# An attention and snake kernel on one core: reciprocals of the first chunk on VectorE, one load on another queue, two reordered stages

## The chip, the core and the metric

The kernel runs on one core of a Trainium2 chip. The metric is the device time in microseconds of one execution. A core has five engines that run their own instruction queues in order and wait for each other by semaphores: TensorE (PE; its weight loads are shown apart as PEld), VectorE (DVE), ScalarE (ACT), GpSimd (POOL) and SyncE (SP). SyncE, ScalarE and GpSimd also start DMA transfers. PSUM, where TensorE writes, is used here as four pairs of banks, called slots 0 to 3.

## What is computed

The reference, cut to what matters. The types are float32.

```python
# q, k, v: (8, 12, 448, 64)
def rmsnorm(x, g):
    return x / np.sqrt(np.mean(x * x, axis=-1, keepdims=True) + 1e-06) * g
q_n, k_n = rmsnorm(q, g_q), rmsnorm(k, g_k)
scores = np.matmul(q_n, k_n.transpose(0, 1, 3, 2)) / np.sqrt(64)
attn = np.exp(scores - np.max(scores, axis=-1, keepdims=True))
attn = attn / (np.sum(attn, axis=-1, keepdims=True) + 1e-09)
x = np.matmul(attn, v).transpose(0, 2, 1, 3).reshape(8 * 448, 12 * 64)
# w_in: (768, 2048), w_out: (2048, 768), alpha: (2048,)
h = x @ w_in
g = h + np.sin(alpha * h) ** 2 / (alpha + 1e-09)
out = g @ w_out
```

## The kernel before

The eight batches run one after the other. The 12 heads of a batch make three chunks of four heads; chunk numbers in the code count through all batches (0, 1, 2 are batch 0's, 3, 4, 5 batch 1's). For a chunk, q and k are loaded (`load_qk`), squared, summed (`reduce`), turned into an inverse root by Ln and Exp on ScalarE (`rsqrt`), scaled (`scale`), and transposed on TensorE (`pe_transpose`, chunks 0 to 2) or by DMA (`transpose`). A batch has 21 score tiles, seven for each chunk: TensorE multiplies (L357), ScalarE takes the exponential (L360), and the result goes to `expT`. Sums over the keys are matmuls with ones into `av` (L416, or L404 for the first chunk of later batches); values are matmuls with `vb`. The reciprocal of the sums, `rec`, is made on ScalarE as Exp of minus Ln (L431 and L432, L423 to L425 in later batches). VectorE multiplies values by `rec` into `xT` (L440).

`first_product` multiplies `xT` by `w_in` into `hps` (L468, 96 matmuls): 24 matmuls for the first four of 16 tiles, in the order of `xT`'s six parts 0, 1, 2, 4, 3, 5, and then six for each tile. ScalarE takes the sine (L446) and half of the squares (L451), GpSimd the other squares (L449), and VectorE writes `g_sb` (L454). `second_product` multiplies `g_sb` by `w_out` into `ops`. For all batches but the last its steps (L548, eight quarter-size matmuls each) are spread as fillers through the next batch's attention; for the last batch it runs by itself at the end (L526, 128 matmuls of 384 columns), with copies to `osb` on VectorE (L532) and, for the last half unit, ScalarE (L534), and stores (L516).

The order of the work is written out by hand in strings. `STAGE_0` is batch 0's, `STAGE_1` batch 1's, `STAGE_N` that of all later ones. Each has three parts: the tokens of the attention, the order in which PSUM slots are taken, and the tasks that stand beside the first product (-1 is ahead of its fifth part, i behind its i-th pair of tiles). Tokens, with a chunk's number within the batch (3, 4 and 5 are the next batch's) and often w (0 for q, 1 for k) and a head pair: `q` square, `u` sum of squares, `g` multiply q by the norm weights, `r` inverse root, `k` scale, `p` transposes on TensorE, `t` by DMA, `l` load q and k, `D` a small copy on GpSimd that waits for a chunk's load, `S` one score tile (`S4` with four warm-up matmuls ahead, L352), `o`, `v`, `x`, `y`, `z` a number of key tiles of the ones of the first chunk, its values, the ones, low and high values of the other two chunks, `G` and `L` the spread of the norm weights and of alpha over the partitions, `V`, `W`, `O` loads of v, `w_in` and `w_out` on GpSimd's queue, `F` (also written as a number) and `f` a filler of the current or of the next half tile of the second product.

A batch-0 `rec` of the first chunk is made when the last `o` is through; for chunks 0 to 3 the inverse root lies in a PSUM slot until the scaling is done.

Of the kernel before, what the change touches and what calls it, by code (L numbers as in the profile page):

```python
# [17 lines left out]
try:  # L18
# [12 lines left out]

STAGE_0 = (
    (
        "q000 u000 q010 G q011 q001 u010 g00 u011 r01 g01 D1 u001 k01 r00 k00 q11 u11 O00 q10 V00 p012 "
        "W01 q20 p00 g1 u10 r1 q21 u20 V01 g2 S4 V02 S k11 l3 k10 S1 S1 S4 W00 W02 S u21 r2 p1 S2 S q31 "
        "S3 k21 q30 k20 D2 S S3 o3 l4 g3 S W10 W12 o1 o3 p2 u30 l5 S3 u31 S1 S W11 S4 v7 S S S q40 S S x5 "
        "y3 q41 u41 x1 g4 z4 u40 x1 L r4 y4 O01 q50 z3 r3 O10 "
    ),
    "012311203203310210213023012310321032021321302",
    {-1: 'u50 O11 k30', 0: 'D4 k401', 1: 'k411', 2: 'q51', 3: 'k31 k400 u51', 5: 'k410', 7: 'g5 V12', 8: 't3 V10 V11 t4 l6 l7'},  # L40
)
STAGE_1 = (
    (
        "4 r2 f f k20 1 f f 2 k21 S 1 q31 1 t2 S 1 S 2 S q30 2 S 2 S S 3 f S 3 S 1 f S 1 S 1 u31 2 l5 g3 "
        "S u30 o1 o6 1 r3 V10 2 S f q41 1 f 2 S 2 S 2 q40 S u41 1 v1 v1 S v3 V12 S k31 q50 v2 u40 S 2 S "
        "V11 g5 S z4 x7 y7 r4 z3 g4 k30 "
    ),
    "1320201203203013133213130101301231203123",
    {-1: 'u50 t3', 0: 'k41', 2: 'k40', 5: 'q51', 6: 'l6 t4', 8: 'u51 l7'},
)  # L50
STAGE_N = (
    (
# [16 lines left out]
def kernel(  # L69
# [23 lines left out]
    nc = tc.nc  # L93
    B, H, S, D = q.shape
    D_MODEL = H * D
    D_FF = moe_w_in.shape[1]
    P = 128
    KT = D_MODEL // P
    MT = D_FF // P
# [7 lines left out]
    HALF = D_MODEL // 2  # L107
# [85 lines left out]
            queue.dma_start(out=g_rows[:, i], in_=src.rearrange("(a d) -> a d", a=1))  # L193

    load_qk(0, nc.scalar)
    load_qk(1, nc.scalar)
    load_qk(2)
    nc.gpsimd.dma_start(out=small, in_=moe_alpha.rearrange("(mt p) -> mt p", p=P))
    nc.scalar.preload_act_table_set(EXP_LN)
# [15 lines left out]
    w_out_sb = wpool.tile([P, MT, D_MODEL], BF16)  # L215
    g_sb = gpool.tile([P, MT, 2 * S], BF16)
# [168 lines left out]
    def attend(b, what, tiles=range(NJ)):  # L385
# [3 lines left out]
        kind, both = what.split()  # L389
        both = both == "1"  # L390
        if tiles[0] == 0:
            avs[what] = bank_pair("av")
        av = avs[what]
        pre = presums.get(b) if what == "ones 0" else None
        last = 1 if pre else NJ - 1
        halved = what == "ones 0" and b > 0
# [22 lines left out]
        if kind == "ones":  # L419
            rec = recs[both] = pre.t if pre else rpool.tile([P, 2, S], F32, tag="rec", name="rec")  # L420
            if halved:
                cols = [slice(0, S // 2), slice(S // 2, S)]
                nc.scalar.activation(rec[:, :, cols[0]], av[:, :, cols[0]], ACT.Ln)  # L423
                nc.scalar.activation(rec[:, :, cols[1]], rec[:, :, cols[0]], ACT.Exp, scale=-1.0)
                nc.scalar.activation(rec[:, :, cols[0]], rec[:, :, cols[0]], ACT.Exp, scale=-1.0)  # L425
                for pp in range(2):
                    for qh in range(2):
                        src, dst = (slice((2 * pp + x) * 32, (2 * pp + x) * 32 + 32) for x in (qh, 1 - qh))
                        nc.vector.reduce_sum(rec[dst, :, cols[qh]], rec[src, :, cols[qh]].unsqueeze(3), axis=AX.X)  # L429
            for k in () if halved else ((0, 1), (1, 2)) if both and b == 0 else ((0, 2),):  # L430
                nc.scalar.activation(rec[:, slice(*k)], av[:, slice(*k), :S], ACT.Ln)  # L431
                nc.scalar.activation(rec[:, slice(*k)], rec[:, slice(*k)], ACT.Exp, scale=-1.0)  # L432
            give_back(avs.pop(what))
        else:
            if b not in xT:
                xT[b] = xpool.tile([P, KT, S], BF16, tag="xT", name="xT")
            first = 0 if not both else 2 if kind == "low" else 3
            for k in (slice(0, 1), slice(1, 2)) if both and b == 0 else (slice(0, 2),):
                kts = slice(first + k.start * (1 + both), first + (k.stop - 1) * (1 + both) + 1, 1 + both)
                nc.vector.tensor_mul(xT[b][:, kts, :], av[:, k, :S], recs[both][:, k])  # L440
            give_back(avs.pop(what))
# [56 lines left out]
    def second_product(b):  # L498
# [19 lines left out]
        for unit in units:  # L518
            st = {}

            def whole_array(m, unit=unit, st=st):
                if m == 0:
                    st["ps"] = bank_pair("ops")
                for k, (i, half) in enumerate(unit):
                    c0 = odd * (S + REST) + i * P if i < NT else NT * P
                    nc.tensor.matmul(st["ps"][:, k, :HALF], g_sb[:, m, c0:c0 + P],  # L526
                                     w_out_sb[:, m, half * HALF:(half + 1) * HALF], start=(m == 0), stop=(m == MT - 1))
                if m == MT - 1:
                    n, i = len(unit), unit[0][0]
                    osb = opool.tile([P, 2, HALF], F32, tag="osb", name="osb")  # L530
                    cut = HALF // 2 if unit is units[-1] else HALF
                    nc.vector.tensor_copy(osb[:, :n, :cut], st["ps"][:, :n, :cut])  # L532
                    if cut < HALF:
                        nc.scalar.copy(osb[:, :n, cut:], st["ps"][:, :n, cut:HALF])  # L534
                    give_back(st["ps"])
                    store(osb[:, :n], i, slice(unit[0][1] * HALF, (unit[-1][1] + 1) * HALF))

# [143 lines left out]
```

## Time and profile before

| what | us |
|---|---|
| median of 8 runs | 409.04 (408.04 to 409.95) |
| the profiled execution | 409.95 |
| its span | 408.2 |
| TensorE busy | 391.5 (96%) |
| ScalarE busy | 315.5 (77%) |
| GpSimd busy | 283.6 (69%) |
| VectorE busy | 240.2 (59%) |

The granted TensorE clock is full in all 40 slices of the span. The chain of work that ended last consists of TensorE for 86% of the span; of its lines, L468 has 34% and L548 29%. The other engines appear in the chain mainly in the first 45 us: loads of q and k, GpSimd's squares, VectorE's scalings.

How to read it: times in the timeline are from the span's start. A line gives start, length, engine, source line, the instruction and its tiles, and in brackets how long the engine stood idle before it and what ended that. A line can merge several instructions (x6); its length is then that of the whole run of them. DMA lines give size and the time from issue to landing.

### The profile page before, as it was taken

What the parts mean: (1) busy time and instruction counts of PE and PEld (TensorE: products, weight loads), DVE (VectorE), ACT (ScalarE), POOL (GpSimd) and SP (SyncE); (2) the same over time, 40 slices, a digit from 0 to 9 for tenths busy, and PEclk for the clock granted to TensorE, in tenths of its full rate; (3) what the DMA queues carried; (4) which work ended last, traced back from release to release, by engine and by line L of the source; (5) the groups of instructions that cost most, each with busy time, mean ns of one, the idle gap of its engine ahead of it and who ended that gap; (6) DMA issues with size and microseconds to landing.
All of it is one profiled execution on the core that took longest, in us unless ns stands there. A gap on an engine that the chain in (4) does not pass through costs nothing.

```text
span 408.2 us, 15186 instructions
## 1 busy us (share of the span) xinstructions
PE 391.5 (96%) x6742; PEld 237.6 (58%) x6742; DVE 240.2 (59%) x363; ACT 315.5 (77%) x475; POOL 283.6 (69%) x268
## 2 busy tenths in 40 slices
PE   0998999999999999999999999999999999999995
PEld 0345467655676556755676556755667556765563
DVE  3956675746784476738584575836685484544411
ACT  4797889878997788958898678958898678977500
POOL 4989879897869789588877779597895774004300
PEclk9999999999999999999999999999999999999999
DMA  7999999766186935699076933979046901520022
GB/s 263 194 252 248 211 203 254 198 124 221 31 149 180 161 101 88 181 171 177 3 134 168 200 114 70 178 169 203 3 95 176 166 2 34 95 61 1 2 77 77
DMA packets 67686, 55.44 MB, mean 136 GB/s; under 512 B 41493, under 2 KB 63013, under 8 KB 67621
## 3 DMA queue, kind: packets, MB, share of 16 engines
q1 hardware_dynamic: 56226, 40.97, 43.2%
q0 software_dynamic: 10432, 11.81, 19.1%
q10 hardware_dynamic: 962, 1.70, 1.1%
q8 instruction: 52, 0.85, 0.9%
q14 instruction: 14, 0.11, 0.1%
HBM read 45.62 MB, written 11.01 MB: 139 GB/s over the span
## 4 chain that ended last, share of the span: by engine, by line
PE 86%; POOL 3%; DVE 3%; DMA 3%; issue 2%; ACT 1%; ACTq 0%; SPq 0%; POOLq 0%
PE hps L468 34%; PE ops L548 29%; PE av L416 9%; PE sc L357 7%; PE ops L526 5%; DMA qk<-in_q_dram 2%; POOL sq L281 2%; PE av L404 1%; DMA qk<-in_k_dram 1%; DVE qkn L309 1%; ACT expT L360 1%; DVE rec L429 1%; DVE ms L290 1%; POOL qk L286 1%; POOL w_out_sb L248 1%
## 5 line engine op out<-in xcount | busy, mean ns | idle before, releaser
L360 ACT ACTIVATE expT<-sc 128x896 bf16<-128x896 f32 x168 | 143.6, 917 | 7.1 <-PE sc L357 6.4
L548 PE MATMUL ops<-w_out_sb,g_sb 64*64 64x384 bf16 x3072 | 148.1, 323 | 0.0
L468 PE MATMUL hps<-xT,w_in 128*128 128x448 bf16 x768 | 146.8, 353 | 0.9 <-DVE alpha_sb L232 0.5
L468 PEld LDWEIGHTS <-w_in 128*128 128x128 bf16 x768 | 74.5, 98 | 72.7 <-issue 4.1
L454 DVE SCALAR_TENSOR_TENSOR g_sb<-s,inv_alpha_sb,hps 128x448 bf16<-128x448 f32 x128 | 81.0, 676 | 59.2 <-POOL s L449 58.7
L548 PEld LDWEIGHTS <-g_sb 64*64 64x64 bf16 x3072 | 92.2, 107 | 36.8 <-issue 3.8
L449 POOL TENSOR_TENSOR s<-s 128x448 f32<-128x448 f32 x64 | 59.7, 933 | 64.8 <-ACT s L446 43.0
L446 ACT ACTIVATE s<-hps,alpha_sb 128x448 f32<-128x448 f32 x128 | 74.0, 627 | 37.8 <-PE hps L468 37.4
L309 POOL TENSOR_TENSOR qkn<-qk,inv 128x448 bf16<-128x448 f32 x80 | 73.0, 940 | 24.5 <-issue 17.1
L281 POOL TENSOR_TENSOR sq<-qk 128x896 f32<-128x896 f32 x44 | 73.4, 1680 | 6.0 <-DVE ms L290 2.9
L357 PE MATMUL sc<-qkT 64*64 64x448 bf16 x672 | 60.2, 355 | 0.7 <-ACT expT L360 0.3
L286 POOL TENSOR_TENSOR qk<-qk,gg 128x896 f32<-128x896 f32 (+1 forms) x25 | 50.5, 2021 | 3.1 <-ACT g_sb L278 2.5
L554 DVE COPY osb<-ops 128x384 f32<-128x384 f32 x48 | 26.7, 556 | 38.6 <-PE ops L548 34.2
L290 DVE TENSOR_REDUCE ms<-sq 128x14 f32<-128x896 f32 x44 | 46.4, 1077 | 5.0 <-POOL sq L281 5.0
L440 DVE TENSOR_TENSOR xT<-av,rec 128x896 bf16<-128x896 f32 (+1 forms) x26 | 25.5, 1013 | 25.8 <-ACT rec L432 21.1
L451 ACT ACTIVATE s<-s 128x448 f32<-128x448 f32 x64 | 36.9, 577 | 3.0 <-DVE g_sb L454 0.7
L416 PE MATMUL av<-expT,vb 64*32 64x448 bf16 (+1 forms) x1120 | 38.1, 350 | 0.0
L357 PEld LDWEIGHTS <-qkT 64*64 64x64 bf16 x672 | 21.8, 107 | 13.6 <-issue 6.1
L555 DVE TENSOR_TENSOR osb<-osb,ops 128x384 f32<-128x384 f32 x48 | 26.6, 554 | 1.7
L416 PEld LDWEIGHTS <-vb 64*32 64x32 bf16 (+1 forms) x1120 | 20.1, 95 | 11.4 <-issue 2.2
L429 DVE TENSOR_REDUCE rec<-rec 32x448 f32<-32x448 f32 x28 | 17.1, 610 | 9.7 <-ACT rec L425 9.4
L526 PE MATMUL ops<-w_out_sb,g_sb 128*128 128x384 bf16 x128 | 21.0, 326 | 0.0
(52 smaller groups left out, 184.8 us busy)
## 6 DMA issues: line engine op xcount, KB each, us to landing
qk<-in_q_dram SPq DMA_DIRECT2D x23, 448.0 KB, 5.2
qk<-in_k_dram SPq DMA_DIRECT2D x22, 448.0 KB, 5.5
out_dram<-osb SPq DMA_DIRECT2D x45, 192.0 KB, 2.9
w_out_sb<-in_moe_w_out_dram POOLq DMA_DIRECT2D x4, 768.0 KB, 12.4
w_in<-in_moe_w_in_dram POOLq DMA_DIRECT2D x6, 512.0 KB, 12.2
vb<-in_v_dram POOLq DMA_DIRECT2D x16, 168.0 KB, 7.4
vb<-in_v_dram POOLq DMA_DIRECT2D x8, 224.0 KB, 4.9
out_dram<-osb SPq DMA_DIRECT2D x14, 96.0 KB, 4.0
```

What stands on the lines that cost most here:

```text
L281: nc.gpsimd.tensor_mul(st.sq[w], qk[ci][:, w], qk[ci][:, w])
L286: nc.gpsimd.tensor_mul(x, x, gg.to_broadcast([P, len(heads) * NJ, D]))
L290: nc.vector.reduce_sum(st.ms[:, w, rows], st.sq[w][:, rows], axis=AX.X)
L309: eng.tensor_mul(n[:, :, hi, :], x[:, hi], inv[:, hi].unsqueeze(2).to_broadcast([P, NJ, D]))
L357: nc.tensor.matmul(sc[o:o + 64, hi, :S], qkt[r, 1, j * REST:(j + 1) * REST], qkt[r, 0, :], start=True, stop=True)
L360: nc.scalar.activation(expT[c, j], sc[:, :, :S], ACT.Exp, scale=SCALE)
L416: nc.tensor.matmul(av[o, k, :S], w, x[r, hi, :], start=(j == 0), stop=(j == last))
L446: nc.scalar.activation(s1, hps, ACT.Sin, scale=alpha_sb[:, m, :])
L449: nc.gpsimd.tensor_mul(s2, s1, s1)
L454: nc.vector.scalar_tensor_tensor(g_sb[:, m, (b % 2) * S:(b % 2 + 1) * S], s2, inv_alpha_sb[:, m, :], hps, op0=ALU.mult, op1=ALU.add)
L468: nc.tensor.matmul(ps[:, m % 2, :S], w_in_sb[m * 2 // MT][:, kt, m % (MT // 2) * P:(m % (MT // 2) + 1) * P], x[:, kt, :], start=(kt == ORD ...
L548: nc.tensor.matmul(st["ps"][os, r, :HALF], g_sb[rs, m, c0 + o * 64:c0 + o * 64 + 64], w_out_sb[rs, m, half * HALF:(half + 1) * HALF], star ...
```

## The change

Four things are edited. The loads: chunk 1's k is issued on SyncE, not on ScalarE. The reciprocal of batch 0's first chunk is made by VectorE from PSUM, in four instructions of 128x224, where ScalarE ran Ln and Exp over 128x896. The last half unit of the output takes 32 matmuls of 192 columns into two banks, where it took 16 of 384 into one; VectorE copies one bank and ScalarE the other. `STAGE_0` and `STAGE_1` get new tokens, slots and tasks; `STAGE_N` is as it was.

In batch 0's new order alpha is spread near the start (`L`); both reductions of chunk 1 stand ahead of chunk 0's transposes; three of the four `w_out` loads move into the first product's tasks, the first part of them as the second; the `w_in` loads are spread (`W00`, `W10`, `W01`, `W02`, `W11`, `W12`); the ones of the first chunk end one score tile earlier, its values come in three pieces; chunk 3's inverse root and scaling come ahead of the last score tile and the first product. Warm-up matmuls are 31 instead of 26. Batch 1 keeps 48 fillers and 21 scores.

```diff
 STAGE_0 = (
     (
-        "q000 u000 q010 G q011 q001 u010 g00 u011 r01 g01 D1 u001 k01 r00 k00 q11 u11 O00 q10 V00 p012 "
-        "W01 q20 p00 g1 u10 r1 q21 u20 V01 g2 S4 V02 S k11 l3 k10 S1 S1 S4 W00 W02 S u21 r2 p1 S2 S q31 "
-        "S3 k21 q30 k20 D2 S S3 o3 l4 g3 S W10 W12 o1 o3 p2 u30 l5 S3 u31 S1 S W11 S4 v7 S S S q40 S S x5 "
-        "y3 q41 u41 x1 g4 z4 u40 x1 L r4 y4 O01 q50 z3 r3 O10 "
+        "q000 q010 u000 q011 u010 G q001 u011 L u001 r01 g00 g01 r00 k01 D1 k00 q10 u10 V01 q11 W00 g1 "
+        "q20 q21 l3 u11 p012 V02 r1 p00 k11 g2 k10 W10 S4 S1 S S4 u20 S u21 q30 r2 q31 V00 l4 o1 D2 p1 S4 "
+        "S1 k21 k20 o4 u30 S2 l5 S1 W01 p2 W02 S1 S o2 S1 u31 S S3 S4 S1 g3 v2 S q40 v4 S W11 S2 v1 S2 x1 "
+        "O01 x1 x1 r3 k31 g4 S x3 y3 x1 u40 k30 q41 W12 u41 r4 y4 z5 z1 z1 k400 q51 "
     ),
-    "012311203203310210213023012310321032021321302",
-    {-1: 'u50 O11 k30', 0: 'D4 k401', 1: 'k411', 2: 'q51', 3: 'k31 k400 u51', 5: 'k410', 7: 'g5 V12', 8: 't3 V10 V11 t4 l6 l7'},
+    "031233102103312020230230232032323210132103210",
+    {-1: 'q50 t3 D4', 0: 'O10', 1: 'O00', 3: 'O11', 4: 'u51 k401 u50', 5: 'k411 V10 k410', 7: 't4 l6', 8: 'g5 l7 V12 V11'},
 )
 STAGE_1 = (
     (
-        "4 r2 f f k20 1 f f 2 k21 S 1 q31 1 t2 S 1 S 2 S q30 2 S 2 S S 3 f S 3 S 1 f S 1 S 1 u31 2 l5 g3 "
-        "S u30 o1 o6 1 r3 V10 2 S f q41 1 f 2 S 2 S 2 q40 S u41 1 v1 v1 S v3 V12 S k31 q50 v2 u40 S 2 S "
-        "V11 g5 S z4 x7 y7 r4 z3 g4 k30 "
+        "r2 f f 1 k21 f f k20 q30 3 f 1 S q31 2 g3 t2 2 V12 S 3 S 2 f S f f S 2 S 2 S 2 S 2 V11 S u30 1 "
+        "l5 S 2 o1 o6 1 f S 1 f 2 S 1 f S q41 2 u31 S 2 q40 S 2 S S 1 v5 S v2 u41 u40 g4 q50 z1 S V10 z1 "
+        "z1 S S r3 z1 k31 z1 k30 x7 u50 y2 r4 y1 y4 z2 g5 "
     ),
-    "1320201203203013133213130101301231203123",
-    {-1: 'u50 t3', 0: 'k41', 2: 'k40', 5: 'q51', 6: 'l6 t4', 8: 'u51 l7'},
+    "2310130232323123103030320321301301230123",
+    {0: 'q51 l6', 2: 'k40', 5: 'k41 u51', 7: 't3 l7', 8: 't4'},
 )
...
     load_qk(0, nc.scalar)
-    load_qk(1, nc.scalar)
+    load_qk(1)
     load_qk(2)
...
-            for k in () if halved else ((0, 1), (1, 2)) if both and b == 0 else ((0, 2),):
+            if b == 0 and not both:
+                for k in range(2):
+                    for cols in (slice(0, S // 2), slice(S // 2, S)):
+                        nc.vector.reciprocal(rec[:, k, cols], av[:, k, cols])
+            for k in () if b == 0 and not both or halved else ((0, 1), (1, 2)) if both and b == 0 else ((0, 2),):
...
-                for k, (i, half) in enumerate(unit):
+                n = 2 if unit is units[-1] else len(unit)
+                width = len(unit) * HALF // n
+                for k in range(n):
+                    i, half = unit[0]
                     c0 = odd * (S + REST) + i * P if i < NT else NT * P
-                    nc.tensor.matmul(st["ps"][:, k, :HALF], g_sb[:, m, c0:c0 + P],
-                                     w_out_sb[:, m, half * HALF:(half + 1) * HALF], start=(m == 0), stop=(m == MT - 1))
+                    w0 = half * HALF + k * width
+                    nc.tensor.matmul(st["ps"][:, k, :width], g_sb[:, m, c0:c0 + P], w_out_sb[:, m, w0:w0 + width],
+                                     start=(m == 0), stop=(m == MT - 1))
...
-                    cut = HALF // 2 if unit is units[-1] else HALF
-                    nc.vector.tensor_copy(osb[:, :n, :cut], st["ps"][:, :n, :cut])
-                    if cut < HALF:
-                        nc.scalar.copy(osb[:, :n, cut:], st["ps"][:, :n, cut:HALF])
+                    if unit is units[-1]:
+                        nc.vector.tensor_copy(osb[:, 0, :width], st["ps"][:, 0, :width])
+                        nc.scalar.copy(osb[:, 0, width:], st["ps"][:, 1, :width])
+                    else:
+                        nc.vector.tensor_copy(osb[:, :n], st["ps"][:, :n, :HALF])
```

## The prediction

> **What bounds the kernel now.** I read first where TensorE stops being the limit: busy time by stage.
>
> ```profile
> 14.00:36.99 22.99, 21.53 (x388) 10.36 (x389) 14.24 (x22) 21.92 (x32) 21.73 (x19) 1.00 1.12 250
> 55.86:83.36 27.50, 26.97 (x722) 19.00 (x722) 16.37 (x25) 25.11 (x35) 25.59 (x23) 1.00 0.98 223
> 83.36:101.63 18.27, 18.27 (x101) 9.32 (x104) 10.78 (x16) 13.73 (x25) 15.76 (x16) 1.00 0.64 177
> 101.63:130.28 28.65, 28.65 (x785) 19.80 (x786) 18.44 (x29) 25.91 (x37) 22.69 (x20) 1.00 0.52 107
> ```
>
> Columns: stretch and its length, then busy time of TensorE, its weight loads, VectorE, ScalarE, GpSimd, then the granted clock. From 83.36 on TensorE is never idle: a batch takes 18.27 + 28.65 = 46.92 us, and that plan is not edited. Time can change only before 83.36 and behind the last matmul. In 14.00 to 36.99 ScalarE is busy 21.92 of 22.99 us (much of TensorE's share is warm-ups).
>
> Then the timeline of that part:
>
> ```profile
> 7.35 1.04 ACT L278 ACTIVATE g_sb<-qk 128x448 f32<-128x448 f32 x2 [2.02 <-DMA qk<-in_k_dram]
> ...
> 24.87 0.96 ACT L431 ACTIVATE rec<-av 128x896 f32<-128x896 f32 x1
> ...
> 36.77 0.16 DVE L232 COPY alpha_sb<-aps 128x16 f32<-128x16 f32 x1
> 36.97 0.25 DVE L234 RECIPROCAL inv_alpha_sb<-alpha_sb 128x16 f32<-128x16 f32 x1
> 36.99 6.97 PE L468 MATMUL hps<-xT,w_in 128*128 128x448 bf16 x36 [0.47 <-DVE alpha_sb L232]
> ...
> 44.35 11.51 PE L468 MATMUL hps<-xT,w_in 128*128 128x448 bf16 x60 [0.39 <-DVE g_sb L454]
> ```
>
> The reader sees the chain: k's second half holds up ScalarE 2.02 us, to 7.35; the first exponential starts at 14.78; the 21 last to 34.19 with a reciprocal pair (Ln and Exp, 24.87 to 26.72) among them; the first product starts at 36.99 after 0.47 us for alpha's copy, loses 0.39 us for a bank, and ends at 55.86. The end:
>
> ```profile
> 403.99 0.36 DVE L532 COPY osb<-ops 128x192 f32<-128x192 f32 x1 [2.04 <-PE ops L526]
> 404.38 0.32 ACT L534 COPY osb<-ops 128x192 f32<-128x192 f32 x1 [19.42 <-DVE osb L532]
> ```
>
> and the two transfers that bear on the queue edit, of equal size and issued 0.2 us apart:
>
> ```profile
> qk<-in_q_dram SPq DMA_DIRECT2D x1, 224.0 KB, 3.3
> qk<-in_k_dram ACTq DMA_DIRECT2D x1, 224.0 KB, 5.6
> ```
>
> **The change, part by part.**
>
> *k of chunk 1 on SyncE.* It no longer stands behind k's second half of chunk 0 on ScalarE's queue; on SyncE it stands ahead of chunk 2's q and k, which had to wait for semaphores until 4.46 anyway. The half landed 2.4 us later than its twin on SyncE (7.35 against 4.9). Bounds: no gain (it is first in its queue), or all 2.2 us. I take 0.4, nearer to none: landing 6.95, first reduction of it on VectorE at 7.56 (before 7.96).
>
> *Stage 0, start.* VectorE's order from there, start to start: reduction 0.54, alpha's copy and reciprocal 0.37 (new here), reduction 0.54, four scalings 2.14 (9.16 to 11.30), now both reductions of chunk 1 (2 x 0.99, before one), three copies 0.90. Last copy done at 7.56 + 6.47 + 0.08 = 14.1; four score matmuls (0.49): first exponential 14.65, before 14.78. What the early copies lost, the earlier landing and the inverse root, which is ready sooner, give back.
>
> *Stage 0, ScalarE.* The pair of 1.85 us goes. Chunk 3's inverse root (0.30 + 0.23) comes in before the last exponential; it stood behind the recs before. New waits: scores 6, 8 and 10 take the bank that exponentials 4, 6 and 8 free, and TensorE puts 4, 2 and 1 warm-ups (0.21 each), 16 ones-matmuls (some 0.75) and two sets of 28 transposes (0.89) there, while an exponential takes 0.80. Bounds 0 (it had none there) to 1.5; I take 1.0. So 14.65 + (34.19 - 14.78) - 1.85 + 0.53 + 1.0 = 33.75 for the end of exponential 21, 0.44 earlier.
>
> *Reciprocals on VectorE.* Four of 128x224. The trace has only 128x16 in 0.25 us; a copy of that shape takes 0.16. Low end: one element per 1.04 ns, as copies do, 0.47 us each, 1.9 in all. High end: all of 0.253 grows with the width, 3.5 each, 14.2 in all. Nearest is the copy: 0.09 / 16 = 5.6 ns on top of 1.04, so 6.6 ns x 224 + 0.08 = 1.56 start to start, 6.2 in all. They can start when TensorE has done the ones of chunk 0 (near 23.9, in step with VectorE, whose queue is at 7.56 + 16.04 = 23.6). Done at 30.1; behind them on VectorE stand chunk 3's second reduction (to 31.1) and the first xT (to 32.1). Who waits: chunk 3's inverse root at 32.4 on ScalarE, and its scalings at 33.05. So 0.95 us is cover. Beyond 7.15 us for the four, each further us is a us later at the first product.
>
> [...] The row gives 6.6 ns; no run here shows the wide form.
>
> *Stage 0, end.* Behind exponential 21 TensorE has 12 groups of 8 matmuls (0.20 each, from 120 in 3.03): 33.75 + 0.05 + 2.4 = first product at 36.2. Before it was 34.19 + 2.8, with alpha's matmuls and the 0.47 us that are now moved. Bank 2 comes from chunk 3's last scaling: VectorE 33.05 + 1.06 + 0.99 + 1.06 = 36.2, just there; then a reduction and the four xT (0.54 each) at 37.7, 38.25, 38.8, 39.3; the product asks for them at 37.7, 38.5, 39.3, 40.0. The 24th matmul ends at 40.8 against 41.55, and the 0.39 us is gone too, since the new slots reuse the first bank one tile later: the product ends at 40.8 + 72 x 0.19 = 54.5, plus 0.3 for the later squares on GpSimd: 54.8, **-1.05**.
>
> *Weights.* Up to the last w_in part GpSimd's queue carries the same bytes as before (six w_in, one w_out, v), so that part lands near 44.6 as before, where the product asks for it at 46.0; the third w_in part, now issued near 24 and so at 34.5 to 38.7 by the landings of 10.5 to 14.7, is asked for at 38.5. The part of w_out that stage 1 reads first is issued by task 1, third of four: the queue is empty by then, the part ahead is issued near 42.9 and takes the 7.4 us of the first one before, the next lands 3.8 later (as those at 48.45 and 52.2 did): 54.1, against 54.8. Cover 0.7. If it is gone, TensorE waits at once. I take +0.1; bounds 0 to 2.
>
> *Stage 1.* 48 second-product steps and 21 scores as before, so 27.50 us hold 25.83 of matmuls (48 x 0.325, from 16 matmuls in 0.65; 21 x 0.19; 0.80, 1.33 and 4.10 for ones and values) and 1.67 of waits. Chunk 3's inverse root (0.55) leaves the exponentials, and one group of 8 fewer stands behind the last one (0.2); but the first scores are spread over more fillers, which costs ScalarE some 0.6 that it had not waited, and the second reduction of chunk 5 now stands ahead of the late xT. I take 0; bounds -0.8 and +0.7. GpSimd's moved v and SyncE's loads land under TensorE's 27 us.
>
> *Last unit.* 32 matmuls of 192 columns for 16 of 384: by the slope from 384 (163 ns) to 448 (190) 32 x 79 = 2.54 against 2.60; if each weight load (98 ns) sets the pace, 3.14. I take +0.05. In the built program ScalarE's copy still waits for VectorE's count of the same unit's copy (367, where the unit before is 366), so the two copies stay in series: gain 0. [...]
>
> **The sum.** -1.05 + 0.1 + 0 + 0.05 = -0.9; as the 0.3 of tight matches above (bank 2, xT) is likelier late than early, I take +0.2 more: **-0.7**. The profiled run took 409.95 (span 408.2, 1.75 around it), which becomes 409.25; the median of the runs is 0.91 lower, 409.04, so **408.3**.
>
> **Rivals.**
> 1. *VectorE becomes the bound.* Mechanism: reciprocals, place: chunk 3's root and the four xT. At 7.85 us for the four nothing is left of the gain; with a fixed part of 0.086 (the scalings' 0.553 apart less 448 x 1.04) one element costs 10.4 ns, the four 9.6: -0.7 + 2.45 = +1.75, 410.8. For: VectorE has no gap from 7.6 to 24. Against: the copy's row. From 7.85 it ends slower. Chance 0.21.
> 2. *w_out late.* If the part ahead needs 12.4 (the median of the four), stage 1 starts 4.3 late, of which ScalarE's waits hide little: 411.5. For: two squares and a gate stand before it. Against: an empty queue. Chance 0.07.
> 3. *Nothing comes of it:* k's half lands as before (+0.4) and scores wait 1.5 (+0.5): +0.2, 409.2. Chance 0.2.
> 4. *Stage 1 gains too:* half of its 1.67 comes back: 407.5. Chance 0.12.
>
> The forecast has 0.4, spread from -1.2 to -0.2. 0.2% (0.8 us) is about what can be told from no change here. Faster: 0.11 of rival 4, 0.2 of the forecast, 0.05 of rival 3's other side (landing 2 us sooner): 0.36. Slower: 0.14, 0.06 and 0.05: 0.25. Within: 0.39. Range: 407.3 (rival 4 with a bit of the landing) to 410.6 (short of rival 1's end).
>
> **What would show it.** Right: four reciprocals near 1.6 us each, first exponential near 14.7, first product's first matmul near 36.2, its end near 54.8, next one's start near 82.3, then 46.92 a batch. Wrong: reciprocals of 1.95 or more and VectorE named ahead of hps; a wait for w_out at the start of stage 1; a wait for w_in inside the product; ScalarE's last copy beside VectorE's.

## The result, and the profile after

The changed kernel takes 412.08 us (median of 11 runs), the kernel before 408.93 (median of 32 beside it): 1.0079 times as long, 95% interval 1.0064 to 1.0093, some 3.2 us slower. The profiled execution has a span of 411.5 us against 408.2. Forecast were 408.3 us, in a range of 407.3 to 410.6. Single executions of some of these kernels are 6 to 15 us longer than the others (one of these 11 took 423.43); ratios and intervals leave them out, and of fewer_warm below, whose profiled execution is one, only stage 0 is read.

The same stages as before, by busy time; columns as in the prediction:

```profile
14.00:37.50 23.50, 22.54 (x391) 10.31 (x388) 20.59 (x27) 20.56 (x29) 21.67 (x18) 1.00 1.06 232
56.40:85.97 29.57, 27.28 (x721) 18.81 (x722) 17.69 (x26) 25.14 (x34) 25.43 (x23) 1.00 1.08 234
85.97:104.24 18.27, 18.27 (x100) 9.30 (x104) 10.62 (x16) 13.94 (x25) 15.86 (x16) 1.00 0.30 79
104.24:133.37 29.13, 29.01 (x785) 20.02 (x786) 17.70 (x28) 25.82 (x37) 23.20 (x20) 1.00 0.73 157
```

The clock is full in every stage. ScalarE's work ahead of the first product has gone down (21.92 to 20.56 us) and VectorE's up (14.24 to 20.59), yet the stretch is half a microsecond longer. The second one holds the loss: 29.57 us from the end of the first product to the next one, where it was 27.50. The last two numbers of a line are the busy share of the 16 DMA engines (by the packets' times, so it can pass 1) and GB/s: in these two stretches the DMA engines are full (1.06 and 1.08), as they were before (1.12 and 0.98).

The timeline of the changed kernel, at the places that the prediction named:

```profile
6.74 1.04 ACT L278 ACTIVATE g_sb<-qk 128x448 f32<-128x448 f32 x2 [1.40 <-DMA qk<-in_k_dram]
...
14.47 4.16 ACT L360 ACTIVATE expT<-sc 128x896 bf16<-128x896 f32 x5 [0.95 <-PE sc L357]
...
19.59 1.73 ACT L360 ACTIVATE expT<-sc 128x896 bf16<-128x896 f32 x2 [0.54 <-PE sc L357]
21.87 1.73 ACT L360 ACTIVATE expT<-sc 128x896 bf16<-128x896 f32 x2 [0.55 <-PE sc L357]
22.41 1.08 DVE L290 TENSOR_REDUCE ms<-sq 128x14 f32<-128x896 f32 x1 [0.84 <-POOL sq L281]
23.41 1.14 DVE L341 COPY qkT<-tp 128x896 bf16<-128x896 bf16 x2
23.96 7.58 ACT L360 ACTIVATE expT<-sc 128x896 bf16<-128x896 f32 x9 [0.37 <-PE sc L357]
24.54 5.79 DVE L433 RECIPROCAL rec<-av 128x224 f32<-128x224 f32 x4
...
37.50 9.82 PE L472 MATMUL hps<-xT,w_in 128*128 128x448 bf16 x51
47.71 8.69 PE L472 MATMUL hps<-xT,w_in 128*128 128x448 bf16 x45 [0.39 <-DMA w_in<-in_moe_w_in_dram]
57.30 3.44 PE L557 MATMUL ops<-w_out_sb,g_sb 64*64 64x384 bf16 x80 [0.91 <-DMA w_out_sb<-in_moe_w_out_dram]
71.46 0.47 PE L404 MATMUL av<-expT,ones 64*32 64x224 bf16 x21 [0.71 <-issue]
82.76 1.51 PE L416 MATMUL av<-expT,ones 64*32 64x448 bf16 x53 [0.68 <-issue]
...
407.31 0.36 DVE L540 COPY osb<-ops 128x192 f32<-128x192 f32 x1 [2.08 <-PE ops L534]
407.70 0.32 ACT L541 COPY osb<-ops 128x192 f32<-128x192 f32 x1 [19.46 <-DVE osb L540]
```

k's half lands earlier, the reciprocals take 1.45 us each, and the first exponential starts 0.3 us sooner. Then ScalarE waits three times for scores (and once more, 0.20 us, at 31.74). The first product starts at 37.50 (36.99 before), waits for `w_in`, the second product waits 0.91 us for `w_out`, and twice TensorE stands still for something the profile does not name ("issue"). How far the changed kernel is behind, by the starts of TensorE's blocks:

| start of | before | after | behind |
|---|---|---|---|
| first exponential | 14.78 | 14.47 | -0.3 |
| first product, batch 0 | 36.99 | 37.50 | 0.5 |
| second product, batch 0 | 55.80 | 57.30 | 1.5 |
| first product, batch 1 | 83.30 | 85.90 | 2.6 |
| first product, batch 2 | 130.21 | 133.31 | 3.1 |
| first product, batch 7 | 364.82 | 368.10 | 3.3 |

### The profile page after: what moved, and what is told of

Same layout as the page of the kernel before. It is cut to its first block, busy times and chain, and to the rows that moved or that the text cites. A ratio compares the mean times of both kernels' runs of the same rounds, so it can differ in the third digit from the quotient of the medians.

```text
span 411.5 us, 15231 instructions
## 1 busy us (share of the span) xinstructions
PE 394.3 (96%) x6763; PEld 241.7 (59%) x6763; DVE 245.7 (60%) x367; ACT 314.7 (76%) x473; POOL 283.9 (69%) x268
## 4 chain that ended last, share of the span: by engine, by line
PE 88%; DMA 4%; ACT 2%; DVE 2%; POOL 2%; issue 1%; ACTq 0%; POOLq 0%
PE hps L472 31%; PE ops L557 31%; PE av L416 10%; PE sc L357 8%; PE ops L534 5%; DMA w_out_sb<-in_moe_w_out_dram 3%; ACT expT L360 2%; PE av L404 1%; PE sc L352 1%; DMA qk<-in_k_dram 1%; DVE ms L290 1%; POOL sq L281 1%; DVE qkn L309 1%; PE tp L334 0%; DVE xT L444 0%
## 5 line engine op out<-in xcount | busy, mean ns | idle before, releaser
L557 PEld LDWEIGHTS <-g_sb 64*64 64x64 bf16 x3072 | 94.5, 107 | 36.4 <-issue 3.7
L357 PE MATMUL sc<-qkT 64*64 64x448 bf16 x672 | 61.5, 353 | 0.0
L416 PEld LDWEIGHTS <-vb 64*32 64x32 bf16 (+1 forms) x1120 | 21.1, 95 | 11.3 <-issue 3.0
L534 PE MATMUL ops<-w_out_sb,g_sb 128*128 128x384 bf16 (+1 forms) x144 | 21.0, 308 | 0.0
```

What stands on the lines that cost most here:

```text
L357: nc.tensor.matmul(sc[o:o + 64, hi, :S], qkt[r, 1, j * REST:(j + 1) * REST], qkt[r, 0, :], start=True, stop=True)
L416: nc.tensor.matmul(av[o, k, :S], w, x[r, hi, :], start=(j == 0), stop=(j == last))
L557: nc.tensor.matmul(st["ps"][os, r, :HALF], g_sb[rs, m, c0 + o * 64:c0 + o * 64 + 64], w_out_sb[rs, m, half * HALF:(half + 1) * HALF], star ...
```

## The experiments

Each ratio is to the kernel before, on the same chip, with its 95% interval. "Block waits" are TensorE's waits with no named cause between the second product's start and the next first product. Starts are of the profiled execution, one for each kernel. Between executions they scatter: before, new_stage1, stage1_after and last_unit have the same stage 0, and their first exponentials start at 13.5 to 14.8 us, their first products at 35.3 to 37.0. So a difference of a microsecond or two between the starts of two rows means nothing by itself; lengths of stages say more.

| kernel | ratio | first product | second product | next first product | block waits |
|---|---|---|---|---|---|
| before | 1 | 36.99 | 55.80 | 83.30 | 0.29 |
| after | 1.0079 (1.0064 to 1.0093) | 37.50 | 57.30 | 85.90 | 1.39 |
| old_stage1 | 1.0143 (1.0100 to 1.0186) | 37.10 | 58.22 | 87.46 | 1.60 |
| new_stage1 | 1.0150 (1.0125 to 1.0174) | 35.25 | 57.23 | 87.26 | 1.43 |
| stage1_before | 1.0046 (1.0028 to 1.0065) | 36.98 | 56.50 | 84.22 | 0 |
| stage1_after | 1.0007 (0.9990 to 1.0025) | 35.88 | 54.70 | 83.05 | 1.30 |
| k_sync | 0.9989 (0.9975 to 1.0003) | 35.87 | 54.69 | 82.74 | 0.84 |
| recips | 1.0166 (1.0135 to 1.0197) | 41.88 | 60.70 | 87.86 | 0 |
| last_unit | 1.0015 (0.9990 to 1.0040) | 36.90 | 55.72 | 82.73 | 0 |
| w_out_order | 1.0109 (1.0079 to 1.0139) | 36.24 | 54.52 | 85.16 | 2.10 |
| w_out_early | 1.0061 (1.0037 to 1.0085) | 36.58 | 56.66 | 87.38 | 2.68 |
| fewer_warm | 1.0085 (1.0054 to 1.0116) | 36.52 | | | |
| vector_order | 1.0090 (1.0058 to 1.0122) | 36.96 | 56.45 | 85.79 | 1.95 |
| all_fixes | 1.0082 (1.0057 to 1.0106) | 36.24 | 54.50 | 85.18 | 2.28 |
| block_shift | 1.0196 (1.0169 to 1.0222) | 39.71 | 57.97 | 89.81 | 2.78 |
| no_store | 1.0061 (1.0037 to 1.0086) | 38.17 | 56.45 | 85.69 | 1.52 |
| v_later | 1.0087 (1.0059 to 1.0115) | 37.23 | 56.93 | 84.77 | 0.68 |
| k_sync_align | 1.0014 (0.9998 to 1.0031) | 36.27 | 55.08 | 82.39 | 0 |
| k_alpha | 0.9989 (0.9964 to 1.0015) | 34.92 | 53.74 | 82.77 | 0.65 |
| k_alpha_align | 0.9999 (0.9980 to 1.0018) | 34.61 | 53.78 | 81.95 | 0.89 |

**The two stages apart.** First the plain swap of stage 1's order.

```diff
 # old_stage1, from after; new_stage1 is the same the other way round, from before
-STAGE_1 = the one of after
+STAGE_1 = the one of before
```

> The changed kernel with the order of stage 1 (tokens, slots, tasks beside its first product) taken from the kernel before. Theory A: the new order of stage 1 costs by itself what the stage (28.67 against 27.50 us from the first to the second first-product block) and the attention of batch 2 (29.13 against 28.65) have lost: both come back, ratio to the changed kernel's 1.0079 falls by 1.65 us to 1.0039, some 410.5. Rival B: the loss is handed down from stage 0 (late w_out, transfers that collide), the order of stage 1 is innocent: 1.0079 stays, stage 1 takes 28.5 or more.

> The kernel before with only the order of stage 1 taken from the changed kernel. Theory A: 1.65 us slower than before, ratio 1.004. Rival B: nothing, 1.000 (within 0.001), stage 1 stays at 27.5.

Both were slower than either parent, which neither theory had. In the trace of the first, the second product starts with a wait of 1.85 us for `g_sb`, in the second of 3.10: the swapped order asks first for the PSUM pair that the last tiles of the first product still hold. So the two say nothing of the stages; the swap was made again with the pairs renamed.

```diff
 # stage1_before, from after (stage1_after from before, with the inverse renaming)
-STAGE_1 = the one of after
+STAGE_1 = the one of before, its pairs 0 1 2 3 called 1 3 0 2, in STAGE_N and LAST too
```

> The changed kernel with the order of stage 1 from the kernel before, its four PSUM pairs renamed (in stage 1, in the later stages and at the end) so that the first tile of stage 1 meets the pair that comes free at the same point as in the kernel before; the swap without renaming had TensorE wait 1.85 us there. Theory A: the new order of stage 1 costs 1 us or more by itself: this kernel is at least 1 us faster than the changed one, ratio 1.005 or less. Rival B: the loss in stage 1 comes from what stage 0 hands over (w_out late, loads pushed back into stage 1, TensorE's instruction blocks that come late there): ratio 1.007 or more, with waits that end on nothing the profile names in stage 1.

> The kernel before with the new order of stage 1, pairs renamed likewise (the swap without renaming waited 3.10 us for a pair). Theory A: ratio 1.003 or more, stage 1 of 28.5 us or more without a wait at its start. Rival B: ratio 0.999 to 1.001, stage 1 of 27 to 27.6 us.

The first has 1.0046, within A's bound of 1.005 (though its interval reaches 1.0065) and short of B's 1.007; the second 1.0007, as B has it, but with a stage 1 of 28.35 us in the trace, between B's 27.6 and A's 28.5, of which 1.30 is a block wait. So batch 0's order with the smaller edits loses some 1.9 us without the new stage 1, the new stage 1 by itself next to nothing in the median (0.3 us, interval -0.4 to 1.0), and both together 3.2; whether the missing us is a joint effect or noise the intervals leave open. In the trace stage1_before still waits for `w_out`, but its stage 1 has no unnamed wait and takes 27.72 us:

```profile
56.50 3.44 PE L557 MATMUL ops<-w_out_sb,g_sb 64*64 64x384 bf16 x80 [0.85 <-DMA w_out_sb<-in_moe_w_out_dram]
60.43 0.52 PE L557 MATMUL ops<-w_out_sb,g_sb 64*64 64x384 bf16 x8 [0.49 <-DMA w_out_sb<-in_moe_w_out_dram]
```

**The small edits alone.**

```diff
 # k_sync, from before
-    load_qk(1, nc.scalar)
+    load_qk(1)
 # recips, from before: VectorE's four reciprocals as in after (L430 to L434), nothing else
 # last_unit, from before: whole_array as in after (L525 to L545), nothing else
```

> The kernel before with only the second chunk's k on SyncE's queue. Theory A: the second half of chunk 0's k lands 0.6 us earlier (6.7 against 7.35), the first exponential starts 0.3 to 0.6 earlier and the first product with it: ratio 0.9985 to 0.999. Rival B: chunk 1's reductions or chunk 2's loads, which now stand behind it on SyncE, take the place: 1.000, first exponential at 14.8 or later.

> The kernel before with only the reciprocals of the first chunk's sums on VectorE, in its old order. Theory A: ScalarE's pair (1.85 us) goes, but in the old order the four reciprocals (5.8 us) stand on VectorE ahead of the copies of chunk 2's transposes (25.33 to 26.5), so its scores come some 5 us late and ScalarE waits for them: 3 us or more slower, ratio 1.007 or more; the reordering was needed for this part. Rival B: ScalarE was the bound: 1 to 1.8 us faster, ratio 0.9955 to 0.9975.

> The kernel before with only the last unit of out in two banks. Theory A: the two copies stay one behind the other: ratio 0.999 to 1.001, ScalarE's last copy starts after VectorE's ends. Rival B: they overlap: 0.3 us faster, ScalarE's copy starts within 0.1 us of VectorE's.

k_sync: 0.9989, as A has it, but the interval holds 1. Nor is the earlier landing shown to come from the edit: the second half of chunk 0's k lands at 7.3, 5.8, 6.2, 5.5 and 5.6 us in the five profiles with chunk 1's k on ScalarE's queue (before, new_stage1, stage1_after, recips, last_unit), at 6.1 in k_sync, and at 5.3 to 7.1 in the other fourteen. recips: 1.0166, A by far; TensorE waits for the copies behind the reciprocals:

```profile
30.64 0.41 PE L357 MATMUL sc<-qkT 64*64 64x448 bf16 x4 [4.39 <-DVE qkT L341]
```

So the reciprocals are a loss of 6.8 us in the old order, which the reordering of stage 0 has to hide. last_unit: 1.0015 with an interval that holds A. Its two copies at the end, VectorE's first, do not overlap:

```profile
403.47 0.36 DVE L536 COPY osb<-ops 128x192 f32<-128x192 f32 x1 [2.08 <-PE ops L530]
403.86 0.32 ACT L537 COPY osb<-ops 128x192 f32<-128x192 f32 x1 [19.46 <-DVE osb L536]
```

**ScalarE's waits for scores in stage 0.**

```diff
 # fewer_warm, from after
-        "q20 q21 l3 u11 p012 V02 r1 p00 k11 g2 k10 W10 S4 S1 S S4 u20 S u21 q30 r2 q31 V00 l4 o1 D2 p1 S4 "
-        "S1 k21 k20 o4 u30 S2 l5 S1 W01 p2 W02 S1 S o2 S1 u31 S S3 S4 S1 g3 v2 S q40 v4 S W11 S2 v1 S2 x1 "
+        "q20 q21 l3 u11 p012 V02 r1 p00 k11 g2 k10 W10 S4 S1 S S4 u20 S u21 q30 r2 q31 V00 l4 o1 D2 p1 S "
+        "S k21 k20 o4 u30 S l5 S W01 p2 W02 S S o2 S1 u31 S S3 S4 S1 g3 v2 S q40 v4 S W11 S2 v1 S2 x1 "
 # vector_order: the same, and u30 behind p2
+        "S k21 k20 o4 S l5 S W01 p2 u30 W02 S S o2 S1 u31 S S3 S4 S1 g3 v2 S q40 v4 S W11 S2 v1 S2 x1 "
```

> The changed kernel without the 9 warm-up matmuls ahead of scores 6 to 10 (they compute nothing that is used). Theory A: ScalarE's waits for scores 6, 8 and 10 (0.54, 0.55 and 0.37 us) shrink by 0.84, 0.42 and 0.21 as far as they reach, together 1.1, and the time from the first exponential to the first product (23.0 us) goes to 22.0; as w_out then is awaited longer the time falls by 0.2 to 1: ratio 1.0055 to 1.0075. Rival B: VectorE or the clock holds it: 22.7 or more from the first exponential to the first product.

> The changed kernel without the 9 warm-up matmuls ahead of scores 6 to 10 and with the reduction of chunk 3's k behind the copies of chunk 2's transposes on VectorE (it waits for GpSimd's square there, and the copies behind it). Theory A: ScalarE's waits for scores come from that: from the first exponential to the first product 22.3 to 22.6 us (23.0 in the changed kernel, 23.3 without the warm-ups alone). Rival B: 23.0 or more, since the reduction then comes too late for chunk 3's inverse root or another wait takes its place.

fewer_warm: 23.32 us from the first exponential to the first product: B. The warm-ups only filled a wait for VectorE, which TensorE now spends idle:

```profile
23.56 0.39 PE L352 MATMUL sc<-blank 128*128 128x512 bf16 x1 [1.31 <-DVE qkT L341]
```

vector_order: 23.05, so B by the letter; but its waits for scores have nearly gone, and a new one has come:

```profile
22.56 5.96 ACT L360 ACTIVATE expT<-sc 128x896 bf16<-128x896 f32 x7 [0.26 <-PE sc L357]
28.55 0.57 PE L416 MATMUL av<-expT,vb 64*64 64x448 bf16 x8 [1.08 <-DMA vb<-in_v_dram]
29.36 3.88 ACT L360 ACTIVATE expT<-sc 128x896 bf16<-128x896 f32 x4 [0.85 <-PE sc L357]
```

In one line the reader sees the old wait reduced to 0.26 us, in the next two TensorE waiting for v's load and ScalarE, a moment later, for the score behind it. Without these 0.85 us it would be 22.2. In all_fixes, with the same edit and 0.23 us of that wait, it is 22.65.

**The weights.**

```diff
 # w_out_order, from after
+        "O00 x1 x1 r3 k31 g4 S x3 y3 x1 u40 k30 q41 W12 u41 r4 y4 z5 z1 z1 k400 q51 "
+    {-1: 'q50 t3 D4', 0: 'O01', 1: 'O10', 3: 'O11', 4: 'u51 k401 u50', 5: 'k411 V10 k410', 7: 't4 l6', 8: 'g5 l7 V12 V11'},
 # w_out_early, from after
+        "O00 x1 x1 r3 k31 g4 S x3 y3 x1 u40 k30 q41 W12 O01 u41 r4 y4 z5 z1 z1 k400 q51 "
+    {-1: 'O10 q50 t3 D4', 0: 'O11', 4: 'u51 k401 u50', 5: 'k411 V10 k410', 7: 't4 l6', 8: 'g5 l7 V12 V11'},
 # all_fixes, from vector_order: W12 right behind W11, O00 in place of O01, tasks 0 to 2: 'O01', 'O10', 'O11'
```

> The changed kernel with the quarters of w_out loaded in the order in which they are read (first quarter in stage 0's plan, second in task 0, third in task 1, where the changed kernel has second, third, first). Theory A: the 0.91 us that the second product waits for its first quarter goes, and as the third quarter is first read some 3 us after the first, nothing takes its place: 0.9 us faster than the changed kernel, ratio 1.0057. Rival B: the stage is held by its scores and loses the 0.9 elsewhere, or the third quarter is late too: 1.0075 or more.

> The changed kernel with w_out's quarters in the order in which they are read and issued before GpSimd's late squares: the second right behind the last part of w_in, the third ahead of the first of those squares, the fourth in task 0. In the changed kernel GpSimd's queue moved 20 GB/s from 45 to 48 us (some 200 around it). Theory A: the queue has no such hole, all quarters are there before they are read, the wait of 0.91 us goes and the loads of stage 1 that SyncE issues start sooner: 0.9 to 1.5 us faster than the changed kernel, ratio 1.0042 to 1.0057. Rival B: the waits for instructions in stage 1 take the gain back: 1.007 or more.

> The same with the last part of w_in issued 5 us sooner (right behind the part before it) and the quarters of w_out in the order of reading, in the plan and tasks 0 to 2. Theory A: no wait for w_in inside the first product (0.39 in the changed kernel) and at most 0.3 for w_out (0.91), the second product starts 1.5 to 2 us sooner: ratio 1.003 to 1.005. Rival B: the parts of w_out, whose issue still stands behind GpSimd's squares, stay late: 1.006 or more.

w_out_order and all_fixes went to B, w_out_early came out between the two. w_out_order and all_fixes start the second product 2.8 us sooner than the changed kernel (1.35 and 0.9 of it stand at the first exponential already, by scatter), and then wait 0.87 and 1.05 us for the third quarter and 2.10 and 2.28 for blocks, so that most of it is gone at the next first product. In w_out_early the early quarter shares the queue with the last part of `w_in`, whose wait goes from 0.39 to 1.62 us. These are all_fixes' waits in that stage:

```profile
59.51 1.17 PE L557 MATMUL ops<-w_out_sb,g_sb 64*64 64x384 bf16 x24 [1.05 <-DMA w_out_sb<-in_moe_w_out_dram]
70.39 0.37 PE L404 MATMUL av<-expT,ones 64*32 64x224 bf16 x12 [1.15 <-issue]
82.23 1.31 PE L416 MATMUL av<-expT,ones 64*32 64x448 bf16 x44 [1.13 <-issue]
```

The expectation of w_out_early called the stretch from 45 to 48 us a hole in GpSimd's queue. It is none: in the DMA view of the changed kernel for this window, `q1`, the queue of SyncE, takes all the engines with small packets (under 512 bytes, the DMA transposes of chunk 3, `t3`, issued at 37.40 and 38.78, which the new order has ahead of the product's fifth part and the old one behind the product, with issues at 51.03 and 52.41), and `q0`, GpSimd's queue with the weights, gets what is left:

```profile
DMA packets 876, 0.27 MB, mean 90 GB/s; under 512 B 846, under 2 KB 846, under 8 KB 876
...
q1 hardware_dynamic: 842, 0.21, 126.1%
q0 software_dynamic: 34, 0.06, 10.8%
```

The kernel before has in the same window only weights, at some 210 GB/s:

```profile
q0 software_dynamic: 417, 0.62, 114.6%
```

The weights' queue moves 0.56 MB less, 2.7 us at that rate, which is more than the 1.5 by which the second product is late. That this is what makes `w_out` late is not shown: moving `t3` back was not tried, and in no_store (below), which has `t3` at the same place, the part of `w_out` issued ahead landed after 7.5 us (9.2 in the changed kernel) and the second product did not wait.

**The unnamed waits.**

```diff
 # block_shift, from after: 72 small matmuls while TensorE is idle at the start (slots for both in step, not shown)
-        "q000 q010 u000 q011 u010 G q001 u011 L u001 r01 g00 g01 r00 k01 D1 k00 q10 u10 V01 q11 W00 g1 "
+        "b40 q000 q010 u000 q011 u010 G q001 u011 L b32 u001 r01 g00 g01 r00 k01 D1 k00 q10 u10 V01 q11 W00 g1 "
-            keep_busy(int(token[1:]), blank)
+            keep_busy(int(token[1:]), blank[:, :64])
```

> The changed kernel with 72 more matmuls of 64 columns on TensorE before the first transposes, when it is idle (they compute nothing that is used): 144 more instructions ahead of everything. In all profiles so far TensorE's waits for nothing that is named (after the first product) stand at instruction 188 + a multiple of 256 of its program. Theory A: they are waits for the next block of 256 instructions (16 KB, the packets of the queue named instruction); then they stay at such numbers, which is 72 matmuls earlier in the work, and as no block then lasts under 4.9 us (3.7 to 4.8 now) they sum to 0.7 us or less in stage 1 (1.39 now). Rival B: they belong to the work there (ones matmuls with 224 columns, a semaphore that the profile misses): they stay before the same matmuls, 21 and 53 before the end of their groups.

As A has it, the waits stay at their numbers in the program, not at their places in the work. But the sum is far off: 4.9 us are in two waits, at places in the work where there had been none.

```profile
39.03 0.75 PE L416 MATMUL av<-expT,vb 64*32 64x448 bf16 x20 [2.08 <-issue]
76.30 1.70 PE L557 MATMUL ops<-w_out_sb,g_sb 64*64 64x384 bf16 x17 [2.78 <-issue]
```

Counted over all profiles, there are 29 unnamed waits of 0.2 us or more from 30 us to the next first product's end (fewer_warm left out). Each stands within six instructions of number 188 + n x 256 (LDWEIGHTS and MATMUL counted together), and each ends 2.2 to 2.5 us after a 16 KB packet of the queue named instruction has started. The number of packets agrees with the spacing: that queue, `q8`, has 52 packets with 0.85 MB in the kernel before and 53 with 0.87 MB in the changed one, and 256 goes 52.7 times into the 13484 instructions of TensorE there and 52.8 times into the 13526 here. The packets come one block ahead. In four rows, all us:

| kernel, number | block before entered | packet starts | packet ends | TensorE goes on |
|---|---|---|---|---|
| after, 2236 | 76.23 | 80.29 | 82.17 | 82.76 |
| k_sync, 2236 | 73.23 | 77.52 | 78.47 | 79.78 |
| block_shift, 1980 | 69.28 | 73.84 | 74.94 | 76.30 |
| after, 5052 (batch 3's attention) | 158.86 | 158.88 | 159.87 | no wait |

So, by the last row, a block is asked for at about the time when the one before it is entered (in the later batches the packets of about a quarter of the blocks start earlier, by up to 4 us). Where the packet starts at once, the 2.2 to 2.5 us that TensorE needed from its start are soon enough: no block in these profiles is worked off in less than 2.8 us. Where it starts 4 us late, a block of less than 6.5 us is too short, and those of stage 1, with its small matmuls, last 3.7 to 5.9 without waits. Late are, on the whole, the packets where other queues fill the engines: over the profiles without fewer_warm's, the middle delay is 2.1 us where their packets take all the time of the 16 engines from 0.5 us before the entry to 2 us after it (222 blocks), and 0.0 where they take under a fifth of it (279 blocks). Here is the DMA view of the changed kernel from 76.2 to 80.2 us, between the entry into the block before and the packet's start:

```profile
q0 software_dynamic: 496, 0.42, 65.1%
q1 hardware_dynamic: 380, 0.66, 50.9%
```

Together 116% of the 16 engines, and no packet of `q8`, the instructions. Three runs were to tell the place of the blocks from the traffic.

```diff
 # no_store, from after
-            for jj in range(2):
+            for jj in range(2 if b else 0):
 # v_later, from after: V12, V11, V10 out of stage 1's plan
-    {0: 'q51 l6', 2: 'k40', 5: 'k41 u51', 7: 't3 l7', 8: 't4'},
+    {0: 'V12 q51 l6', 1: 'V11', 2: 'V10 k40', 5: 'k41 u51', 7: 't3 l7', 8: 't4'},
 # k_sync_align, from k_sync: one S4 becomes S1, three S3 and one S4 become S
```

> The changed kernel without the stores of the first batch's output (these rows stay unwritten); all else as it was. Theory A: what makes the blocks late in stage 1 is the traffic of the other queues, of which these stores (SyncE, 72 to 81 us) are the last large part: the waits at 82.8 fall below 0.3, the packet of that block starts within 2 us of the crossing of the block before (4.1 now), ratio 1.0055 to 1.007. Rival B: the stores do not matter: 1.0075 or more, waits as before.

> The changed kernel with the three loads of batch 2's v moved from stage 1's plan (72 to 74 and 84 us) to tasks 0 to 2 of the first product behind it. Theory A: the blocks are late because of the traffic beside them: with 0.3 MB less, the packet of the block that is asked for near 76 us starts within 2.5 us (4.1 in the changed kernel) and the wait near 82.8 goes: ratio 1.005 to 1.007. Rival B: other traffic (transposes, stores, q and k) is enough: waits as before, 1.0075 or more.

> The kernel before with the second chunk's k on SyncE's queue and 16 of the 26 warm-up matmuls ahead of scores left out (no place where ScalarE waited for a score): 32 instructions fewer ahead of stage 1, so that its blocks begin 16 matmuls later in the work, where by the trace of the k kernel alone they last 5.4, 4.3, 5.3, 5.8 and 7.1 us instead of 5.4, 4.8, 4.7, 5.7 and 4.7. Theory A: the waits for blocks in stage 1 (0.84 and 0.45 there, 0.29 in the kernel before) sum to 0.5 or less: ratio 0.9965 to 0.9985. Rival B: the place does not decide, only the traffic: 0.9985 or more, waits of 0.8 or more; or the clock falls without warm-ups.

no_store and v_later both lost the wait near 82.8, with that packet 2.8 and 3.1 us after the block before was entered (4.1 in the changed kernel): in the trace A's direction, though not the 2 and 2.5 us that were set. Without the stores the ratio is within A's, but a wait of 0.83 came at 76.73; v_later pays later (0.76 us for `g_sb` at 104.91, and 29.78 us for batch 2's attention), and its ratio is B's. k_sync_align has no block wait at all, as A has it, and is no faster, 1.0014, as B has it, with a clock that did not fall (1.0 in the profiled execution, 0.999 in k_sync's): the next wait is alpha's copy, behind reductions that wait for GpSimd.

```profile
36.27 6.97 PE L468 MATMUL hps<-xT,w_in 128*128 128x448 bf16 x36 [1.31 <-DVE alpha_sb L232]
```

last_unit, whose program up to the last batch is that of before, had no block waits either, where before has one of 0.29: executions of one program differ. That traffic and place both count fits these runs; one execution of each does not settle how much each.

**A faster version?** The two parts of the change that had looked free, put into the old order.

```diff
 # k_alpha, from k_sync (k_alpha_align: the same from k_sync_align); slots in step, not shown
-        "q000 u000 q010 G q011 q001 u010 g00 u011 r01 g01 D1 u001 k01 r00 k00 q11 u11 O00 q10 V00 p012 "
+        "q000 u000 q010 G q011 q001 u010 L g00 u011 r01 g01 D1 u001 k01 r00 k00 q11 u11 O00 q10 V00 p012 "
-        "y3 q41 u41 x1 g4 z4 u40 x1 L r4 y4 O01 q50 z3 r3 O10 "
+        "y3 q41 u41 x1 g4 z4 u40 x1 r4 y4 O01 q50 z3 r3 O10 "
```

> The kernel before with the second chunk's k on SyncE's queue and alpha's transpose, copy and reciprocal at the start of stage 0 (behind the first chunk's first reduction of k) instead of its end. Theory A: the wait for alpha ahead of the first product (0.47 us in the kernel before, 0 to 1.31 in its variants) is gone for good: from the first exponential to the first product 21.6 to 21.8 us, ratio 0.9975 to 0.999. Rival B: the two small operations delay the first scalings and exponentials by as much, or the reductions behind which alpha stood hold the product's xT instead: 0.999 or more.

> The same without the 16 warm-up matmuls that were left out before. Theory A: no waits for blocks in stage 1 (0 in the run with the same place of the blocks), no wait for alpha: ratio 0.996 to 0.998 and lower than the kernel with alpha alone. Rival B: the fewer warm-ups bring no gain over the kernel with alpha alone: within 0.0007 of it.

The first product starts at 34.92 and 34.61, 2 us sooner than in before (1.2 and 1.3 of it stand at the first exponential already), 21.35 and 21.13 us after the first exponential, and without a wait for alpha. But the next first product starts only 0.5 and 1.35 us sooner, and the ratios, 0.9989 and 0.9999, cannot be told from 1: the first lies in A's range, the second in neither's, with a block wait of 0.89 where A had none. k_alpha gives it back here:

```profile
72.84 0.38 PE L357 MATMUL sc<-qkT 64*64 64x448 bf16 x2 [0.90 <-DMA qkT<-qkn]
79.81 1.14 PE L416 MATMUL av<-expT,ones 64*32 64x448 bf16 x39 [0.65 <-issue]
```

Among the seven kernels with the old stage 0 but for small edits (recips and new_stage1 aside), the first product's start varies by 2.4 us and the next one's by 1.35. No version was shown to beat the kernel before.

## Why the prediction was wrong

Right were the parts that the trace of before showed directly, but for the first, which is luck:

- *k on SyncE:* landing 6.7 (forecast 6.95), first exponential 14.47 (14.65). The landing scatters from 5.3 to 7.3 between executions on either queue, so the 7.35 from which the gain of 0.4 was taken was one draw, the latest of twenty, and no run shows a gain from the queue.
- *Reciprocals:* 5.79 us for four, against 6.2 by the copy's row: 224 elements in 1.45 us are at most 6.5 ns each, where the row gave 6.6. They lie in the cover that was named, and VectorE is not the bound through them (rival 1).
- *Bank wait of 0.39:* gone. *Last unit:* 21.00 us for the last product against 20.96 (+0.04, forecast +0.05; by the prediction's own slope a matmul of 192 columns is 82 ns, not 79), and the copies in series, as the wait in the program said. What two copies from two banks side by side would give was not tried.
- *46.92 a batch later on:* four of six intervals; the other two have 0.49 and 0.18 more.

Wrong were three terms, the first by its size and two by what they left out:

1. *"Stage 0, ScalarE": 1.0 us of waits for scores.* Measured: 34.96 - 14.47 = 20.49 us to the end of exponential 21; without waits it would be 19.41 - 1.85 + 0.53 = 18.09, so 2.40, past the bounds of 0 to 1.5; ScalarE's rows show 1.66 of it as idle time. Seven other profiles with this stage 0 (in two of them with other places for the loads of `w_out`) have 20.7 to 21.3 us, so it is no accident of one execution. The places were right (scores 6, 8, 10). What was left out is that VectorE's copies of the transposes stand behind reductions that wait for GpSimd's squares (0.84 us at 22.41). fewer_warm showed that the warm-ups, which the estimate counted, were filling; vector_order that moving one reduction removes most of the wait, and that v's load is next. First product: +0.5 where -0.8 was forecast; from the first exponential it is 23.0 to 23.8 us in all eight but block_shift, 21.55 in the forecast, and 21.7 to 22.2 in four profiles with the old stage 0 (23.5 in last_unit).
2. *"Weights": +0.1, w_out at 54.1 us.* The wait was 0.91, with a landing at 57.3. The product ended 1.6 us later than forecast, but that quarter landed 3.2 later: the load ahead of it was issued at 44.29 (forecast 42.9) and took 9.2 us (7.4), so a cover of 0.7 became a lack of 0.9. The step took the queue ahead for empty and the landing times of before; it did not count the transposes of `t3`, which the change moves into the first product and which hold the DMA engines from 45 to 48 us, and the last `w_in` part, issued 4 us later than before behind a square. That the transposes made the 9.2 is argued from the packets, not tried. This is rival 2 (411.5 us, given 0.07), at a fifth of its price of 4.3 us; that its time was nearly met is chance.
3. *"Stage 1: I take 0, bounds -0.8 and +0.7".* 28.60 us from the second product's start to the next first product against 27.50: +1.10. The unnamed waits account for it (1.39 against 0.29). Less these waits and those for DMA inside it, stage 1 takes 26.9 to 27.7 us in 17 of the 20 profiles, with either order (new_stage1 and block_shift, which stood still for 3 us at or in it, have 28.6 and 29.0, fewer_warm 29.7): the 0 held for all but the waits for instructions. Before had one of them in plain view, and the sum of the stage's waits took no notice of it:

```profile
80.33 1.14 PE L416 MATMUL av<-expT,ones 64*32 64x448 bf16 x40 [0.29 <-issue]
```

*The sum:* -0.7 against +3.2. Of the 3.3 us in the two profiles, 0.5 is there at the first product (forecast -0.8), 1.0 more at the second product, 1.1 more in stage 1, and 0.7 in later batches, of which 0.5 in batch 2, where two matmuls at number 4028 of the program (188 again) start 0.47 us apart.

Open is how much of the 3.2 us a single edit holds: the runs give 1.9 us for stage 0 and the small edits without the new stage 1, and 1.3 (by difference) for the new stage 1 on top of it, where by itself it cost 0.3. No edit of the changed kernel brought its time back to that of before; the effect of `t3` was seen, not tried.

## What to carry to other kernels

An operation taken from the busy engine was worth here only what the queues around it let through: four hidden reciprocals saved ScalarE 1.85 us, and the order that hid them made scores and weights late for more (2.40, 0.39 and 0.91). When a step is moved, list its DMAs and ask which transfers it meets in its new place: the DMA engines were full here in the first 80 us (busy share 1.05 before, 1.08 after), and of the 2.8 us by which w_out_order and all_fixes started the second product sooner, 0.7 were left at the next first product, behind waits of 2.97 and 3.33 us for `w_out` and for instructions. Before a gain is taken from one wait at the start of a kernel, see how far that wait scatters between executions. And look for waits without a name at equal distances in TensorE's program: here its instructions came by DMA too, in 53 packets with 0.87 MB.

## What the hardware showed

- TensorE's instructions came in 16 KB packets of 256 during the run, 52 of them in the kernel before and 53 in the changed one. A wait for one ended 2.2 to 2.5 us after its packet's start, 29 times out of 29; the packet started 0 to 1.7 us after the block before was entered in most of the later batches, and 1.8 to 4.8 us after in most of stage 1. Single waits reached 2.78 us. 72 idle matmuls at the start, which move the borders of the blocks, cost some 4.8 us by the ratios (1.0196 against 1.0079); in the profiled executions the span is 3.5 us longer and the waits for blocks are (4.86 against 1.39).
- DMA transposes with 0.21 MB took the DMA engines from 45 to 48 us (126% of the 16 engines' time by their packets), in which the weights' queue moved 0.06 MB; in the kernel before, without them, it moved 0.62.
- VectorE's reciprocal of 128x224 from PSUM took 1.45 us (5.79 for four), against 1.08 us for a reduction of four times as many elements (128x896, mean of 44).
